# Rows 3 and 4 of a banded-attention and feed-forward kernel: row 3's x transposed by DMA, q and k loaded ahead of dilated v

## The chip, the cores and the metric

One core of one Trainium2 chip. The metric is the time of one execution in microseconds, as the device reports it; the median of 3 runs of the kernel before is 307.24 us (306.99 to 307.94).

The engines go by these names: PE is TensorE's matrix multiply and PEld its weight load, DVE is VectorE, ACT is ScalarE, POOL is GpSimd, SP is SyncE (which here issues DMAs only; its queue is SPq in the profile). Each engine works through its own instructions in order, and waits where one of them needs another engine's or a DMA's result.

## The reference, cut to what matters

```python
def _attn_ref(q, k, v):                   # (8, 8, 576, 64): batch, head, token, dim
    scores = scale * np.matmul(q, k.transpose(0, 1, 3, 2))
    rel = pos[:, None] - pos[None, :]
    mask_plain = (rel >= 0) & (rel < 32)                      # heads 0 to 3
    mask_dil = (rel >= 0) & (rel < 128) & (rel % 4 == 0)      # heads 4 to 7
    ...
    attn = np.exp(scores)
    attn = attn / (np.sum(attn, axis=-1, keepdims=True) + 1e-09)
    return np.matmul(attn, v)

def _moe_ref(x, w_in, w_out):             # x: (4608, 512), w_in: (512, 2048)
    r = np.maximum(x @ w_in, 0.0)
    return (r * r) @ w_out

def reference(q, k, v, moe_w_in, moe_w_out):
    attn_out = _attn_ref(q, k, v)
    x = attn_out.transpose(0, 2, 1, 3).reshape(8 * 576, 8 * 64)
    return _moe_ref(x, moe_w_in, moe_w_out)
```

So: banded attention, in heads 0 to 3 over the last 32 tokens ("sliding"), in heads 4 to 7 over every fourth of the last 128 ("dilated"), and then two dense layers over all 4608 tokens with a squared ReLU between them.

## The kernel before, in words

**Rows and chunks.** A *row* is one batch entry: 576 tokens of attention, rows 0 to 7. The dense layers work in chunks of 512 tokens, 0 to 8. While the attention of row b runs, the dense work of chunk b - 1 is dealt out between its pieces, so that TensorE always has something to do: `moe_gen(c)` is a generator, and each `pump(n)` takes n *steps* from it. From chunk 2 on, a chunk has 60 steps: 32 for the first layer (two per block of 128 hidden features, each two matmuls of 128x512 into a PSUM tile `ph`, after the second of them ScalarE's ReLU into `rt` and VectorE's square into `g`), and 28 for the second, a Strassen scheme with PSUM tiles `pa`, `pb`, `pc` (four matmuls of 128x256 to a step). The `ph`, `pa`, `pb`, `pc` tiles share four PSUM buffers, `rt` has three in SBUF. What each engine does, in which order, follows from the order of the program text alone.

**One row of attention.** Scores: two groups of sliding heads (`s_sliding`, tiles `ps`, from `QKTp`), two of dilated heads (`s_dilated`, `pz`, from `QKTd`), each followed by ScalarE's exponentials and VectorE's masks. Values: three groups of sliding blocks (`av_sliding`, `pav`, from `vp`), four of dilated ones (`av_dilated`, `paw`, from `vd`), each normalized by VectorE into `xs` or `xd`. Then x has to lie with features on partitions, in `xT`, which holds the last four rows. Two ways:

- by TensorE (`attn_values`, rows 0 to 3): `x_sliding` and `x_dilated` transpose blocks into PSUM (`px`, `py`), and ScalarE copies them into `xT`;
- by the DMA's crossbar (`attn_values_by_dma`, rows 4 to 7): SyncE issues transposing DMAs, the sliding ones straight into `xT`, the dilated ones into `yd`, from where ScalarE copies them (`x_from`, some steps later).

**What a row needs beforehand.** Its q and k: GpSimd's DMAs bring sliding q and k (`ns`) and put dilated q and k as fp16 in DRAM (`dd`); VectorE brings the sliding ones into order of tokens (`nr`, `by_token`), SyncE writes them to DRAM (`dp`, `keep_sliding_qk`) and reads both back transposed (`QKTp<-dp`, `QKTd<-dd`, two DMAs each, k and then q). Its v: SyncE loads `sv` (sliding) and `sd` (dilated) as fp32, GpSimd casts them into `vp` and `vd` (3 and 4 casts). Blocks overlap, so a *halo* of partitions 96 to 127 (sliding) or 64 to 127 (dilated) is copied down within `vp` and `vd`: by ScalarE in rows 0 to 2, by DMA on SyncE in rows 3 and 4 (`vp<-vp`, `vd<-vd`); in rows 5 to 7 the sliding one is a VectorE copy (line 196) put off to the end of the stage before (`at_end`, called in the Strassen scheme after the fourth product into `pa`, step 56).

`after_transposes(b)` is a tiny GpSimd copy that makes GpSimd wait for row b's transposes, so that no load of the next row is issued ahead of them.

**Where rows 3 and 4 stand.** The main loop has two parts: rows 2 and 3 in the old manner, rows 4 to 7 in the new. In the first, `turn_and_load` issues, for the next row: copy by token and `dp`, `sv`, `sd`, the four transposes, and all seven casts. Row 2 calls it after its third `av_sliding` (step 42 of its chunk's 64); row 3 calls it from `attn_scores` after the last scores (step 24 of 60). Row 3 begins its scores at step 12. In the second part a row begins its scores at step 3; `copied` (copy by token and `dp`) comes after the third `av_sliding`, for row 4 after the second; `first` (`sv`) after the first `x_dilated_by_dma`; `second` (transposes, then `sd`, the sliding casts, the halo at the end) after the other one. The dilated casts of a row from 5 on are made in the row itself, after GpSimd has issued the next row's loads.

Of the kernel before, what the change touches and what calls it, by code (L numbers as in the profile page):

```python
# [13 lines left out]
P = 128  # L14
# [3 lines left out]
def kernel(  # L18
# [9 lines left out]
    nc = tc.nc  # L28

    B, H, S, D = q.shape  # L30
# [16 lines left out]
    NB = S // QB  # L47
    PADP = P - QB
# [41 lines left out]
    vp = [const.tile([P, NB, HH, D + 2], FP16, name=f"vp{r}") for r in range(2)]  # L90
# [18 lines left out]
    def load_sliding_qk(b):  # L109
        n = natp.tile([P, HH, 9 * D], FP16, name=f"ns{b}", tag="n")  # L110
        for i, s in ((1, k), (0, q)):
            nc.gpsimd.dma_start(
                out=n[64 * i : 64 * (i + 1)],
                in_=s[b, 0:HH].rearrange("h (p j) d -> p h (j d)", j=9),
            )
        return n
# [8 lines left out]
    def load_sliding_v(b):  # L125
        vv = v[b, 0:HH].rearrange("h (m p) d -> p h m d", p=QB)
        if b == 0:
            for m in range(NB):
                nc.sync.dma_start(out=sv[PADP:P, :, m, :], in_=vv[:, :, m, :])  # L129
        else:  # L130
            for h in (0, 2):
                nc.sync.dma_start(out=sv[PADP:P, h : h + 2], in_=vv[:, h : h + 2])

    def load_dilated_v(b, eng):
        vv = v[b, HH:H].rearrange("h (i c) d -> i h (c d)", c=DIL)
        for t in range(2):
            eng.dma_start(out=sd[P - QD[t] : P, t, :, :], in_=vv[Q0D[t] : Q0D[t] + QD[t]])
# [29 lines left out]
    def cast_sliding_v(b, ms=range(0, NB, 2)):  # L167
        for m in ms:
            nc.gpsimd.tensor_copy(  # L169
                vp[b % 2][:, m : m + 2, :, 0:D], sv[:, :, m : m + 2, :].rearrange("p h m d -> p m h d")  # L170
            )

    def cast_dilated_v(b):
        for t in range(2):
            p0 = 64 * t
            for c in range(0, DIL, 2):
                nc.gpsimd.tensor_copy(  # L177
                    vd[b % 2][p0:P, t, c : c + 2, :, 0:D],
                    sd[p0:P, t, :, D * c : D * (c + 2)].rearrange("p h (c d) -> p c h d", d=D),
                )  # L180
# [11 lines left out]

    at_end: list = []

    def halo_sliding_at_end(b):
        nc.vector.tensor_copy(
            vp[b % 2][0:PADP, 1:NB, :, 0:D], vp[b % 2][P - PADP : P, 0 : NB - 1, :, 0:D]
        )

    def halo_sliding_by_dma(b):  # L200
        nc.sync.dma_start(out=vp[b % 2][0:PADP, 1:NB], in_=vp[b % 2][P - PADP : P, 0 : NB - 1])

    def halo_dilated_by_dma(b):
        nc.sync.dma_start(out=vd[b % 2][0:64, 1], in_=vd[b % 2][64:P, 0])

    def cast_v(b):
        cast_sliding_v(b)
        cast_dilated_v(b)


    def keep_dilated_qk(b):
        d = dpool.tile([2, HH * CL, DIL * D], FP16, name=f"dd{b}", tag="dd")
        for i, src in ((1, k), (0, q)):
            nc.gpsimd.dma_start(
                out=d[i].rearrange("(r i) x -> r (i x)", i=4),
                in_=src[b, HH:H].rearrange("h (r i) d -> (h r) (i d)", i=16),
                max_dma_last_dim=4096,
            )
        return d
# [10 lines left out]
    def transpose_sliding(b, dp):  # L230
        for i in (1, 0):
            nc.sync.dma_start_transpose(out=QKTp[b % 2][:, i, :, PADP:], in_=dp[i])

    def transpose_dilated(b, dd):
        for i in (1, 0):
            nc.sync.dma_start_transpose(out=QKTd[b % 2][:, i, :, KPAD:], in_=dd[i])
# [4 lines left out]
    def after_transposes(b):  # L241
        nc.gpsimd.tensor_copy(seen, QKTd[b % 2][:, 0, 1, KPAD : KPAD + 1])
# [25 lines left out]
    for m, w, pad in (  # L268
# [5 lines left out]
            out=lo_[:, 0:w], in0=relf[:, 0:w], scalar1=-pad - 0.5, scalar2=None, op0=ALU.is_gt  # L274
# [9 lines left out]
    for r in range(2):  # L284
        nc.vector.tensor_scalar(
            out=vd[r][:, 0, :, :, D],
# [220 lines left out]
    def moe_gen(c):  # L507
        g = hidden(c)
        yield from mm1_gen(c, g, c > 1)
        yield from (mm2_strassen_gen if c > 1 else mm2_gen)(c, g)  # L510
# [10 lines left out]
    def pump(n):  # L521
        for _ in range(n):
            while pending:
                try:
                    next(pending[0])
                    break
                except StopIteration:
                    pending.pop(0)
# [184 lines left out]
    def attn_scores(b, gap, less=0, hooks={}):  # L713
        for hp in range(2):
            s_sliding(b, hp)
            if hp in hooks:
                hooks[hp]()
            pump(gap)
        for g in range(2):
            s_dilated(b, g)  # L720
            if 2 + g in hooks:
                hooks[2 + g]()
            if g and b < 3:
                halo_sliding(b, 0)
            pump(gap - less)

    def attn_values(b, gap, wide=False, then=None):
        xs = x_tiles(b)
        for mp in range(3):
            av_sliding(b, mp, xs)  # L730
            if b < 3:
                if mp < 2:
                    halo_sliding(b, mp + 1)
                else:
                    halo_dilated(b, 0)
            if then and b == 2 and mp == 2:
                then()
            pump(gap + (b == 1 and mp == 0))
        x_sliding(b, 0, xs, wide)
        if b < 3:  # L740
            halo_dilated(b, 2)
        pump(gap)
        av_dilated(b, 0, 0, xs)
        if then and b == 1:
            then()
        pump(gap)
        x_sliding(b, 1, xs, wide)
        pump(gap)
        av_dilated(b, 0, 1, xs)
        pump(gap)  # L750
        for a in range(2):
            av_dilated(b, 1, a, xs)
            pump(gap)
        x_dilated(b, 0, xs, wide)
        pump(gap)
        x_dilated(b, 1, xs, wide)

    def attn_values_by_dma(b, then):
        xs = x_tiles(b)
        for mp in range(3):  # L760
            av_sliding(b, mp, xs)
            if mp == (2 if b > 4 else 1):
                then[0]()
            pump(3)
        x_sliding_by_dma(b, xs)
        ys = []
        for t in range(2):
            for a in range(2):
                av_dilated(b, t, a, xs)
                pump(4 + 2 * (a > t))  # L770
            ys.append(x_dilated_by_dma(b, t, xs))
            then[1 + t](ys[t])
        pump(6)
        x_from(b, 0, ys[0])
        pump(7)
        x_from(b, 1, ys[1])
# [38 lines left out]
    ns = load_sliding_qk(2)  # L815
# [43 lines left out]
    def turn(b, n):  # L859
        return keep_sliding_qk(b, by_token(b, n))  # L860

    for b in range(2, 4):
        pending.append(moe_gen(b - 1))
        nxt = b + 1
        after_transposes(b)
        ns = load_sliding_qk(nxt)
        if b == 2:
            cast_v(b)
        dd = keep_dilated_qk(nxt)
        if b == 3:  # L870
            halo_sliding_by_dma(b)
            halo_dilated_by_dma(b)

        def turn_and_load():
            dp = turn(nxt, ns)
            load_sliding_v(nxt)
            load_dilated_v(nxt, nc.sync)
            transpose_sliding(nxt, dp)
            transpose_dilated(nxt, dd)
            cast_v(nxt)  # L880

        pump(22 if b == 2 else 12)
        attn_scores(b, 4, 0, {3: turn_and_load} if b == 3 else {})
        attn_values(b, b, False, turn_and_load)
        pump(1000)

    for b in range(4, B):
        pending.append(moe_gen(b - 1))
        nxt = b + 1
        if nxt < B:  # L890
            after_transposes(b)
            ns = load_sliding_qk(nxt)
            dd = keep_dilated_qk(nxt)
        if b > 4:
            cast_dilated_v(b)
        else:
            halo_sliding_by_dma(b)
        halo_dilated_by_dma(b)
        dps = []

        def copied():
            if nxt < B:
                dps.append(turn(nxt, ns))

        def first(y):
            if nxt < B:
                load_sliding_v(nxt)

        def second(y):
            if nxt < B:  # L910
                transpose_sliding(nxt, dps[0])
                transpose_dilated(nxt, dd)
                load_dilated_v(nxt, nc.sync)
                nc.gpsimd.tensor_copy(seen, y[:, 0, 0, 0:1])
                cast_sliding_v(nxt)
                at_end.append(lambda: halo_sliding_at_end(nxt))

        pump(3)
        attn_scores(b, 3)
        attn_values_by_dma(b, (copied, first, second))  # L920
        pump(1000)
    pending.append(moe_gen(B - 1))
# [32 lines left out]
```

## Time and profile before

| what | value |
|---|---|
| median of 3 runs | 307.24 us (306.99 to 307.94) |
| the profiled execution's own time | 306.99 us |
| its span in the profile | 304.6 us |
| granted TensorE clock | 1.00 |
| VectorE's square, `g<-rt` 128x512 (line 329) | 446 ns, 144 of them |
| VectorE's halo copy of `vp` (line 196) | 485 ns, 3 of them |
| GpSimd's casts `vp<-sv`, `vd<-sd` | 675 and 695 ns |
| `dp<-nr`, issue to landing, median | 4.1 us |
| `QKTp<-dp` and `QKTd<-dd`, issue to landing, median | 4.5 and 3.9 us |
| `xT<-xs` and `yd<-xd`, issue to landing, median | 4.0 and 2.9 us |

Times in the profile are microseconds from the start of the span. A line of the timeline has an instruction group's start, its length, engine, source line, operation, written tile and read tiles; "x8" is a number of instructions run together, and a bracket at the end gives the idle time of the engine ahead of it and what ended that. Matmuls are pipelined, so the length of a group reaches a little into the next one. The stages lie like this: row 3's with chunk 2 from 95 us, row 4's from 128, row 5's from 158, row 6's from 188, row 7's from 218; from 248 on there is dense work only (chunks 7 and 8).

### The profile page before, as it was taken

The numbers are of one execution on the slowest core, as the hardware profiler recorded it, in microseconds if no ns is written. First come the engines' busy times: TensorE is split into PE (matmuls) and PEld (weight loads), VectorE is DVE, ScalarE is ACT, GpSimd is POOL, SyncE is SP. The second block draws the span as 40 slices with busy tenths as digits, with TensorE's granted clock in tenths as the row PEclk, the third lists the DMA queues.
The fourth block names the chain that finished last, engine by engine and source line by source line (L and its number), as shares of the span: only waits on it lengthen the run. The fifth ranks groups of instructions, "written<-read, shape, count | busy, mean of one in ns | idle before, by whom it ended". The sixth has DMA issues, their size and how long they took to land.

```text
span 304.6 us, 6894 instructions
## 1 busy us (share of the span) xinstructions
PE 286.2 (94%) x2760; PEld 192.7 (63%) x2760; DVE 210.4 (69%) x437; ACT 173.2 (57%) x293; POOL 63.7 (21%) x112
## 2 busy tenths in 40 slices
PE   1888999799999799999999999999999999999994
PEld 1554554454554358855888997558756975785583
DVE  7684549658861689479938994999499924824651
ACT  2856647478835783395349635953495346425620
POOL 4481008101611610530027002600230000000000
PEclk9999999999999999999999999999999999999999
DMA  7999994999699999997899989998983230003013
GB/s 115 196 195 213 210 172 79 195 227 226 132 198 148 261 176 213 174 250 144 140 155 273 174 142 196 270 182 169 165 246 41 39 132 8 2 1 138 2 36 103
DMA packets 77471, 46.77 MB, mean 154 GB/s; under 512 B 58432, under 2 KB 69184, under 8 KB 77440
## 3 DMA queue, kind: packets, MB, share of 16 engines
q1 hardware_dynamic: 68688, 32.71, 50.5%
q0 software_dynamic: 8752, 13.63, 26.4%
q8 instruction: 21, 0.34, 0.5%
q14 instruction: 10, 0.08, 0.1%
HBM read 36.70 MB, written 16.52 MB: 175 GB/s over the span
## 4 chain that ended last, share of the span: by engine, by line
PE 74%; DMA 17%; DVE 4%; POOL 1%; issue 1%; SPq 1%; ACT 1%; POOLq 0%; DVEq 0%
PE ph L305 35%; PE pa L382 15%; PE pb L382 7%; DMA sv<-in_v_dram 6%; PE po L450 5%; DMA wi<-in_moe_w_in_dram 5%; PE pc L382 4%; DMA QKTp<-dp 3%; DMA ns<-in_q_dram 2%; PE paw L659 2%; PE ps L588 1%; PE pav L643 1%; PE pz L613 1%; PE py L690 1%; SPq L129 1%
## 5 line engine op out<-in xcount | busy, mean ns | idle before, releaser
L305 PE MATMUL ph<-xT,wi 128*128 128x512 f16 (+1 forms) x640 | 134.2, 359 | 0.7 <-ACT xT L696 0.7
L328 ACT ACTIVATE rt<-ph 128x512 f16<-128x512 f32 x144 | 86.2, 608 | 44.6 <-PE ph L305 41.8
L305 PEld LDWEIGHTS <-wi 128*128 128x128 f16 x640 | 68.2, 114 | 45.9 <-issue 0.6
L329 DVE TENSOR_TENSOR g<-rt 128x512 f16<-128x512 f16 x144 | 62.7, 446 | 37.8 <-ACT rt L328 36.6
L382 PEld LDWEIGHTS <-g 128*128 128x128 f16 x448 | 43.0, 98 | 6.3 <-DVE g L329 0.2
L382 PEld LDWEIGHTS <-gs 128*128 128x128 f16 x336 | 32.5, 98 | 3.7
L450 PE MATMUL po<-wo,g 128*128 128x512 f16 x128 | 33.1, 379 | 0.0
L382 PE MATMUL pb<-wt,g 128*128 128x256 f16 x224 | 28.1, 273 | 0.0
L382 PE MATMUL pa<-wt,gs 128*128 128x256 f16 x224 | 27.1, 273 | 0.0
L169 POOL CAST vp<-sv 128x512 f16<-128x512 f32 x24 | 15.4, 675 | 55.4 <-DMA sv<-in_v_dram 42.7
L409 DVE TENSOR_TENSOR ov<-pb,ov 128x512 f32<-128x512 f32 x14 | 9.7, 692 | 23.7 <-PE pb L382 18.6
L398 ACT COPY ov<-pa 128x512 f32<-128x512 f32 x14 | 8.2, 587 | 28.0 <-PE pa L382 28.0
L177 POOL CAST vd<-sd 128x512 f16<-128x512 f32 (+1 forms) x32 | 21.4, 695 | 10.2 <-DMA sd<-in_v_dram 9.6
L631 DVE TENSOR_TENSOR xd<-paw,rcp_d 80x512 f16<-80x512 f32 (+1 forms) x32 | 21.9, 685 | 1.1
L572 ACT ACTIVATE AT<-ps 128x576 f16<-128x576 f32 x32 | 19.2, 657 | 3.0 <-PE ps L588 2.6
L572 ACT ACTIVATE AT<-pz 128x576 f16<-128x576 f32 x32 | 19.8, 693 | 1.3 <-PE pz L613 1.1
L575 DVE TENSOR_TENSOR AT<-AT,maskd 128x576 f16<-128x576 f16 x32 | 18.8, 613 | 1.9 <-ACT AT L572 0.8
L575 DVE TENSOR_TENSOR AT<-AT,maskp 128x576 f16<-128x576 f16 x32 | 15.0, 479 | 6.7 <-ACT AT L572 5.1
L631 DVE TENSOR_TENSOR xs<-pav,rcp_p 96x512 f16<-96x512 f32 x24 | 16.5, 687 | 0.8
L659 PEld LDWEIGHTS <-AT 128*128 128x128 f16 x256 | 11.9, 98 | 7.3 <-issue 2.4
L398 ACT COPY ou<-pa 128x512 f32<-128x512 f32 x14 | 8.2, 586 | 13.8 <-PE pa L382 13.8
L450 PEld LDWEIGHTS <-g 128*128 128x128 f16 x128 | 10.4, 97 | 8.3
(81 smaller groups left out, 274.7 us busy)
## 6 DMA issues: line engine op xcount, KB each, us to landing
sv<-in_v_dram SPq DMA_DIRECT2D x14, 288.0 KB, 5.4
dp<-nr SPq DMA_DIRECT2D x12, 288.0 KB, 4.1
out_dram<-ou SPq DMA_DIRECT2D x6, 512.0 KB, 4.0
out_dram<-ov SPq DMA_DIRECT2D x6, 512.0 KB, 4.8
sd<-in_v_dram SPq DMA_DIRECT2D x8, 320.0 KB, 6.1
ns<-in_k_dram POOLq DMA_DIRECT2D x8, 288.0 KB, 6.9
ns<-in_q_dram POOLq DMA_DIRECT2D x8, 288.0 KB, 8.3
sd<-in_v_dram SPq DMA_DIRECT2D x8, 256.0 KB, 5.5
```

The source lines that it names most:

```text
L169: nc.gpsimd.tensor_copy(vp[b % 2][:, m : m + 2, :, 0:D], sv[:, :, m : m + 2, :].rearrange("p h m d -> p m h d"))
L177: nc.gpsimd.tensor_copy(vd[b % 2][p0:P, t, c : c + 2, :, 0:D], sd[p0:P, t, :, D * c : D * (c + 2)].rearrange("p h (c d) -> p c h d", d=D),)
L305: nc.tensor.matmul(ph[:, t0:t1], wi4[ffc // 4][:, dmk, :, ffc % 4], xT[:, dmk, x0 : x0 + t1 - t0], start=(dmk == 0 and t0 == 0), stop=(dmk ...
L328: nc.scalar.activation(rt, ph[:], ACTF.Relu)
L329: nc.vector.tensor_mul(g[:, ffc, :], rt, rt)
L382: nc.tensor.matmul(banks[bank][:, t], a(k, t), b(k), start=(new and t == 0 and k == 0), stop=(k == HF - 1), skip_group_check=True,)
L398: nc.scalar.copy(ot, banks[A])
L450: nc.tensor.matmul(po, g[:, ffc, t * P : (t + 1) * P], wo[ffc // 4][:, ffc % 4, :], start=(ffc == 0), stop=(ffc == NFF - 1),)
L572: nc.scalar.activation(AT[:, u, 0:UW], ps[:, :, 0 : UW // 2], ACTF.Exp, scale=scale)
L575: nc.vector.tensor_mul(AT[:, u, 0:UW], AT[:, u, 0:UW], mask)
L631: nc.vector.tensor_tensor(out=x, in0=pv, in1=rb, op=ALU.mult)
L659: nc.tensor.matmul(pav[:, e, h * (D + 2) : h * (D + 2) + D + 1], AT[:, 4 + h, off : off + P], vd[b % 2][:, t, 2 * a + e, h, 0 : D + 1], st ...
```

## The change

Row 3 goes over from the first manner to the second, and the loop's first part becomes straight code for row 2 alone.

- `turn_and_load` (for row 3, called in row 2): the four transposes are issued ahead of the two `sd` loads, and GpSimd makes only the sliding casts; the dilated casts of row 3 come in row 3's own stage.
- Row 3: scores from step 6, then 3 steps between pieces; x by the crossbar with `attn_values_by_dma`; the copy by token for row 4 after the third `av_sliding` (again step 24), `sv` of row 4 behind the first dilated x transpose, the transposes for row 4 and its `sd` behind the second (step 45). Its sliding halo is a VectorE copy after the second group of sliding scores, its dilated halo stays a DMA. The last x copy comes at step 58 of 60 (in rows 4 to 7 at 55).
- Row 4: dilated casts in its own stage; sliding halo by VectorE at the end of row 3's stage in place of a DMA; the copy by token for row 5 after the third `av_sliding`, not the second.

Rows 5 to 7 are as before. The change in the code:

```diff
-    def halo_sliding_at_end(b):
+    def halo_sliding_at_once(b):
         nc.vector.tensor_copy(
             vp[b % 2][0:PADP, 1:NB, :, 0:D], vp[b % 2][P - PADP : P, 0 : NB - 1, :, 0:D]
         )
-
-    def halo_sliding_by_dma(b):
-        nc.sync.dma_start(out=vp[b % 2][0:PADP, 1:NB], in_=vp[b % 2][P - PADP : P, 0 : NB - 1])
...
-            if then and b == 2 and mp == 2:
+            if then and b > 1 and mp == 4 - b:
                 then()
...
-            if mp == (2 if b > 4 else 1):
+            if mp == 2:
                 then[0]()
...
-    for b in range(2, 4):
-        pending.append(moe_gen(b - 1))
-        nxt = b + 1
-        after_transposes(b)
-        ns = load_sliding_qk(nxt)
-        if b == 2:
-            cast_v(b)
-        dd = keep_dilated_qk(nxt)
-        if b == 3:
-            halo_sliding_by_dma(b)
-            halo_dilated_by_dma(b)
-
-        def turn_and_load():
-            dp = turn(nxt, ns)
-            load_sliding_v(nxt)
-            load_dilated_v(nxt, nc.sync)
-            transpose_sliding(nxt, dp)
-            transpose_dilated(nxt, dd)
-            cast_v(nxt)
-
-        pump(22 if b == 2 else 12)
-        attn_scores(b, 4, 0, {3: turn_and_load} if b == 3 else {})
-        attn_values(b, b, False, turn_and_load)
-        pump(1000)
-
-    for b in range(4, B):
+    pending.append(moe_gen(1))
+    after_transposes(2)
+    ns = load_sliding_qk(3)
+    cast_v(2)
+    dd = keep_dilated_qk(3)
+
+    def turn_and_load():
+        dp = turn(3, ns)
+        load_sliding_v(3)
+        transpose_sliding(3, dp)
+        transpose_dilated(3, dd)
+        load_dilated_v(3, nc.sync)
+        cast_sliding_v(3)
+
+    pump(22)
+    attn_scores(2, 4)
+    attn_values(2, 2, False, turn_and_load)
+    pump(1000)
+
+    for b in range(3, B):
...
-        if b > 4:
-            cast_dilated_v(b)
-        else:
-            halo_sliding_by_dma(b)
+        cast_dilated_v(b)
         halo_dilated_by_dma(b)
...
-                at_end.append(lambda: halo_sliding_at_end(nxt))
-
-        pump(3)
-        attn_scores(b, 3)
+                at_end.append(lambda: halo_sliding_at_once(nxt))
+
+        pump(6 if b == 3 else 3)
+        attn_scores(b, 3, 0, {1: lambda: halo_sliding_at_once(b)} if b == 3 else {})
         attn_values_by_dma(b, (copied, first, second))
         pump(1000)
```

## The prediction

> **What bounds the kernel now.** I read the page's engine shares first, then TensorE's order of work around the edited rows, then SyncE's queue beside it, then busy time by stage. The page and the list of waits:
>
> ```profile
> PE 286.2 (94%) x2760; PEld 192.7 (63%) x2760; DVE 210.4 (69%) x437; ACT 173.2 (57%) x293; POOL 63.7 (21%) x112
> ...
> PE ps L588 <- DMA QKTp<-dp: 2.0, 2, 1.6
> ```
>
> TensorE is the bound: a change counts by the work it takes from TensorE and by the waits it makes or ends there. One of the few waits after the start is the sliding scores' (`ps`) for the transposed q and k, 1.6 us of it once. TensorE's timeline puts it at the head of row 3:
>
> ```profile
> 95.08 5.34 PE L305 MATMUL ph<-xT,wi 128*128 128x512 f16 x24
> 102.04 0.43 PE L588 MATMUL ps<-QKTp 64*128 64x96 f16 x12 [1.62 <-DMA QKTp<-dp]
> ...
> 115.91 0.42 PE L672 MATMUL px<-ident,xs 96*128 96x96 f16 x6
> 116.17 1.48 PE L382 MATMUL pc<-wo,g 128*128 128x256 f16 x12
> ...
> 219.90 0.43 PE L588 MATMUL ps<-QKTp 64*128 64x96 f16 x12 [0.38 <-DMA QKTp<-dp]
> ```
>
> Row 3 runs its 12 dense steps (24 matmuls), idles 1.62 us, and starts its scores at 102.04. Row 7 shows the same wait at 219.90, 0.38 us. SyncE's queue says what is late for row 3 (start, us spent issuing):
>
> ```profile
> 85.14 1.14 SPq L224 DMA_DIRECT2D dp<-nr  x2
> 86.37 3.42 SPq L132 DMA_DIRECT2D sv<-in_v_dram  x2
> 89.89 3.72 SPq L137 DMA_DIRECT2D sd<-in_v_dram  x2
> 93.70 5.71 SPq L232 DMA_TRANSPOSE QKTp<-dp  x2
> 99.50 3.04 SPq L236 DMA_TRANSPOSE QKTd<-dd  x2
> ```
>
> The transposes queue behind both loads of v. By stage, from one row's first score to the next row's (rows 3, 4, 5, 6):
>
> ```profile
> 95.08:129.68 34.60, 32.70 (x323) 22.44 (x322) 24.27 (x48) 19.22 (x34) 11.39 (x19) 1.00 1.17 196
> 129.68:159.54 29.86, 29.86 (x299) 21.50 (x300) 23.51 (x49) 18.09 (x31) 4.65 (x9) 1.00 0.89 173
> 159.54:189.46 29.92, 29.92 (x351) 26.91 (x352) 24.76 (x49) 17.99 (x31) 7.67 (x13) 1.00 1.01 194
> 189.46:219.90 30.44, 30.05 (x289) 20.61 (x289) 25.02 (x50) 18.22 (x31) 7.11 (x13) 1.00 0.94 194
> ```
>
> (The first begins at row 3's first dense step. Columns: length, busy PE, PEld, DVE, ACT, POOL, clock, DMA share, GB/s.) In rows 4 to 6, TensorE is full; row 3's stage is what the change can shorten. The clock is 1.00 throughout.
>
> **The change part by part.** *Row 3's x leaves TensorE.* 28 transposes (two `px` groups of 6, two `py` of 8) go. From the start of each group to the next matmul they take 0.26, 0.32, 0.29 and 0.34: 1.21 us. ScalarE's copies out of them (0.59 to 0.69) become copies from `yd` (1.1 to 1.3), about 1.1 us more in a stage where ScalarE has some 15 us free: nothing. Four crossbar transposes on SyncE replace them; in row 4 they land 2.6 to 4.4 us after issue, three dense steps or more ahead of use, as `x_from` comes late: nothing directly.
>
> The VectorE: DVE Perf Modes page of the Trainium skill (Rules for kernel authors) speaks against this: a 128x128 transpose belongs on TensorE when PSUM will do. Its table gives 390 ns there and 1309 ns by the crossbar, so by an estimate from it the row's 18 blocks would be 7 us of TensorE against 24 us of DMA. The trace's 1.21 us for the whole row decides; the rule leaves out that here TensorE is the full engine.
>
> *Row 3's scores from step 6; the transposes ahead of dilated v.* Six steps from 95.24 (the chain has 1.30 us for 6 matmuls, so 2.60) make TensorE ready at 97.84. When does q land? `dp` for k is issued at 85.14 and lands after 6.3 us, at 91.5; the transposes can't issue before. Row 2's pattern had `dp` directly ahead of the transposes but for a 0.5 MB store: first issued at 61.99, second landed at 63.9 + 4.0 = 67.9, 5.9 us on. That gives 97.4 here, no wait. The other bound: only the issue moves, from 93.70 to 91.5, and the landing of 102.04 with it, to 99.8: 2.0 us of wait. The 576 KB of sliding v in 256-byte pieces still lie ahead, worse than row 2's store, so I take a middle 98.75: **0.9 us of wait (0 to 2.0)**. QKTd landed 2.8 us behind QKTp before, and row 3's dilated scores come 3.6 us behind the first: no second wait.
>
> *Row 4's q and k come later.* Before, row 3 issued them at step 24; now at step 45, behind `dp`, the x transposes and sliding v, as rows 4 to 6 do. There the second QKTp landed 28.05, 29.46 and 30.40 us after the row's own first score (157.8, 189.0, 219.86), and the next scores came 29.9 us after it: 1.7 and 0.5 us early, then 0.4 late. Row 3 has three steps less between its scores and row 4's, since it starts at step 6, not 3: 29.92 - 1.30 = 28.62. VectorE sets when `yd` issues (it runs without a gap from 160.50 to past 182): three or so products `g` (0.4 each) fall before the scores, but the halo copy (0.49) and one `ou` add (0.67) come in ahead of the last `xd`, and some 0.4 idles early, +0.35 in all. By the nearest rows, 5 and 6, the landing is at 29.93 + 0.35 = 30.3; by row 4, which had its copy earlier and no casts beside, 28.4. I take 30.1: **1.5 us of wait (0 to 2.2)**.
>
> *Row 4 and the moved v work.* Row 4's copy moves from step 18 to 21, so row 5 loses row 4's 1.7 us margin and stands between +0.5 and -0.4: **0.1 us (0 to 0.4)**. Four dilated casts each for rows 3 and 4 (2.9 us a row on GpSimd) move behind the next loads' issue; GpSimd is idle there and row 5's do the same. The sliding halo moves from SyncE (0.61 to 0.76 of issue) to VectorE: 0.49 us each. Row 3's waits for the `vp` casts, over at 99.96, while VectorE reaches it about 4 us after the scores, near 102.7: no stall. Behind it stand `g` products; three `rt` and four `ph` buffers cover about 3 us; uncovered it would cost its own excess. Row 4's waits at the end of row 3's stage for the casts behind `yd`; such waits (up to 2.4 us) held nobody in rows 5 to 7. `vd<-vd` waits in SyncE ahead of `dp`, but `dp` isn't due for 5 us more. Row 3's dilated v, issued after four transposes (about 1.5 us each from 91.5) near 98, lands some 5 us later (rows 5 to 7: 4.4 to 4.8), near 103; its casts take 2.9, and the first dilated product comes 11.8 us after the scores (row 5: 171.26 against 159.47), near 110.5: hidden.
>
> **Sum.** From 95.24 to row 4's scores at 129.75 are 34.51 us. After: 2.60 + 0.9 + 28.62 + 1.5 = 33.62, a gain of 0.89; less 0.1 for row 5: **0.8 us**. The gross is 3.29 (1.62 and 0.28 of ended waits, 1.21 of transposes, the rest slips), of which two new waits give most back. The profiled execution took 306.99 (span 304.6), which makes 306.2; the median is 0.25 higher, which makes **306.4**.
>
> **The rivals.** *A, forecast:* both waits remain in part, 305.4 to 307.4, chance 0.5.
> *B, the crossbar is in time:* QKTp follows `dp` as in row 2 and row 4's lands by row 4's pattern, no waits: gain 3.3, 304.0; with a remnant of 0.5, 304.5. For it: the two quick cases. Against: rows 5 and 6 slip nearer to zero margin each time. 0.2.
> *C, slower by late q and k at each row's head:* row 3's landing at its late bound (2.0), row 4's at 2.2, and rows 5 and 6 each at row 7's 0.4 with SyncE's queue slipping: 3.29 - 5.0 = -1.7, so 308.9. It decides once the waits at the heads add to over 3.3 us. For it: the DMA engines' share is already 1.17 in row 3's stage, and row 7 waits. Against: in rows 5 and 6 the slip stays under 0.4. 0.25.
> *D, the turn doesn't advance anything:* the transposes still wait for `dp` of q (93.1) and stand behind sliding v, landing near 101: wait 3.2, gain about -1.4 to 0; 307.8. 0.05.
>
> On the crossbar's rate, Advanced Engine Details and Errata in the skill (X-Bar Transpose (TRN2)) expects 350 to 400 GB/s; by an estimate from that, two transposes of 288 KB would take 1.6 us. Between 99 and 104 the trace moved 215 to 255 GB/s in full microseconds of transposes (143 in one), which speaks for C rather than B.
>
> **How the numbers follow.** About 0.3%, 0.9 us, can't be told from no change. A's gains run from -0.2 to 1.8, somewhat under half of them over 0.9: 0.22 of faster, with B 0.42. Same: 0.28 from A, 0.05 from C's mild end, 0.02 from D: 0.35. Slower: the rest of C and D, 0.23. The range leaves B's best and C's worst outside: 304.6 to 308.5; the forecast's own is 305.4 to 307.4.
>
> **What would show it.** No `px` or `py` groups after row 2; `sd` issued behind QKTd; first `ps` of row 3 near 98.8 with a wait of 0 to 2; row 4's `ps` near 128.9 with a wait of 0.5 to 2.2 on QKTp; later stages 29.9 to 30.4. I am wrong if row 4's wait is gone or above 2.5, if TensorE waits on `vp`, `vd` or `xT` in row 3, or if VectorE stalls at the halo copy.

## The result and the profile after

| measurement | before, median | changed, median | ratio, 95% interval |
|---|---|---|---|
| first, 4 runs each | 307.24 us (306.99 to 307.94) | 306.24 us (306.05 to 306.43) | 0.9964 [0.9946, 0.9982] |
| repeat on chip 7 (c1_again), 29 and 12 runs | 305.16 us | 305.76 us | 1.0018 [0.9984, 1.0052] |
| repeat on chip 1 (e4_again2), 23 and 12 runs | 306.10 us | 305.99 us | 1.0007 [0.9971, 1.0042] |

The first measurement (its chip isn't on record) is 1.0 us faster, 0.4%; the forecast was 306.4. The two repeats, whose runs spread more (303 to 310 us), show no gain; their intervals allow from 0.9 us faster to 1.6 us slower. So the number was met, but the change is worth about 1 us at most, and perhaps nothing. The traces say more, because single stages are steadier than the whole.

TensorE's timeline of the changed kernel around row 3 and the heads of rows 4 and 5:

```profile
93.66 2.75 PE L302 MATMUL ph<-xT,wi 128*128 128x512 f16 x12
96.82 0.43 PE L585 MATMUL ps<-QKTp 64*128 64x96 f16 x12 [0.41 <-DMA QKTp<-dp]
...
111.33 0.42 PE L656 MATMUL paw<-vd,AT 128*128 128x65 f16 x8 [0.43 <-DVE xs L628]
...
127.19 0.43 PE L585 MATMUL ps<-QKTp 64*128 64x96 f16 x12 [0.82 <-DMA QKTp<-dp]
...
137.85 0.41 PE L640 MATMUL pav<-vp,AT 128*128 128x65 f16 x8 [0.37 <-DVE xs L628]
```

SyncE's queue there, first for row 3's q, k and v, then for row 4's:

```profile
83.72 1.14 SPq L221 DMA_DIRECT2D dp<-nr  x2
84.96 3.17 SPq L132 DMA_DIRECT2D sv<-in_v_dram  x2
89.57 4.66 SPq L229 DMA_TRANSPOSE QKTp<-dp  x2
94.33 2.97 SPq L233 DMA_TRANSPOSE QKTd<-dd  x2
97.35 1.32 SPq L137 DMA_DIRECT2D sd<-in_v_dram  x2
...
113.07 3.82 SPq L698 DMA_TRANSPOSE xT<-xs  x2
116.99 1.23 SPq L705 DMA_TRANSPOSE yd<-xd  x1
118.27 1.22 SPq L132 DMA_DIRECT2D sv<-in_v_dram  x2
119.74 1.99 SPq L705 DMA_TRANSPOSE yd<-xd  x1
121.85 2.78 SPq L229 DMA_TRANSPOSE QKTp<-dp  x2
```

And by stage, as before the change (row 3's first dense step to row 4's first score, then score to score for rows 4 and 5; the columns are those of the prediction):

```profile
93.66:127.19 33.53, 31.78 (x296) 21.32 (x295) 24.91 (x50) 19.40 (x32) 9.09 (x16) 1.00 0.95 189
127.19:157.62 30.43, 30.06 (x294) 21.25 (x294) 25.44 (x50) 17.64 (x30) 7.04 (x13) 1.00 1.01 200
157.62:188.72 31.10, 30.37 (x347) 26.70 (x347) 24.60 (x49) 17.78 (x31) 7.22 (x13) 1.00 0.93 189
```

The transposes of row 3's x are gone from TensorE, its wait of 1.62 us has shrunk to 0.41, and the first stage is 1.07 us shorter than the 34.60 of before. But row 4 now begins with a wait of its own, TensorE waits for VectorE's `xs` in both rows, and rows 4 and 5 are longer than the 29.79 and 29.93 of before (by the starts of the first scores). Both traces span 304.6 us. The changed one reached row 3 1.42 us sooner (93.66 against 95.08). That may be chance: the code up to there is the same but for the places of a few DMAs and casts, and ten of the traces in the table below reached row 3 anywhere from 93.6 to 95.1 us, and one (d1_casts_act4, after a stretch at half clock) at 97.8. The traced execution of e3_qk_first_act was a slow one (318.39 us, granted clock 0.984), so its stages aren't in the table.

### The profile page after: what moved, and what is told of

It is laid out like the page before. It is cut to its first block, busy times and chain, and to the rows that moved or that the text cites. A ratio compares the mean times of both kernels' runs of the same rounds, so it can differ in the third digit from the quotient of the medians.

```text
span 304.6 us, 6841 instructions
## 1 busy us (share of the span) xinstructions
PE 286.2 (94%) x2732; PEld 191.3 (63%) x2732; DVE 214.0 (70%) x439; ACT 173.0 (57%) x291; POOL 64.9 (21%) x113
## 4 chain that ended last, share of the span: by engine, by line
PE 68%; DMA 12%; DVE 9%; ACT 6%; issue 3%; SPq 1%; POOL 1%; POOLq 0%
PE ph L302 26%; PE pa L379 15%; DMA ns<-in_q_dram 7%; PE pb L379 7%; PE po L447 6%; PE pc L379 4%; DVE g L326 3%; DMA QKTp<-dp 3%; ACT AT L569 3%; PE paw L656 2%; ACT rt L325 2%; DMA QKTd<-dd 2%; DVE AT L572 2%; PE ps L585 1%; PE pf L513 1%
## 5 line engine op out<-in xcount | busy, mean ns | idle before, releaser
L326 DVE TENSOR_TENSOR g<-rt 128x512 f16<-128x512 f16 x144 | 64.2, 460 | 34.1 <-ACT rt L325 32.9
L379 PE MATMUL pa<-wt,gs 128*128 128x256 f16 x224 | 26.9, 273 | 0.0
L177 POOL CAST vd<-sd 128x512 f16<-128x512 f32 (+1 forms) x32 | 22.7, 736 | 12.7 <-DMA sd<-in_v_dram 12.2
L572 DVE TENSOR_TENSOR AT<-AT,maskd 128x576 f16<-128x576 f16 x32 | 19.7, 642 | 2.6 <-ACT AT L569 1.5
L902 POOL COPY seen<-yd 128x1 f16<-128x1 f16 x4 | 0.8, 191 | 73.6 <-DMA yd<-xd 73.6
```

What stands on the lines that cost most here:

```text
L177: nc.gpsimd.tensor_copy(vd[b % 2][p0:P, t, c : c + 2, :, 0:D], sd[p0:P, t, :, D * c : D * (c + 2)].rearrange("p h (c d) -> p c h d", d=D),)
L326: nc.vector.tensor_mul(g[:, ffc, :], rt, rt)
L379: nc.tensor.matmul(banks[bank][:, t], a(k, t), b(k), start=(new and t == 0 and k == 0), stop=(k == HF - 1), skip_group_check=True,)
L572: nc.vector.tensor_mul(AT[:, u, 0:UW], AT[:, u, 0:UW], mask)
```

## The experiments

The stages of the traces, in us, for the whole section. "To row 4" starts at row 3's first dense step; the others run from the row's first score to the next row's, and "rest" from row 7's first score to the end. Each kernel has one trace. The ratio is that of the times to the kernel before on the same chip: 7 for the c runs, 3 for the d runs, 1 for the e runs. The changed kernel itself ran on chips 7 and 1, not on 3.

| kernel | to row 4 | row 4 | row 5 | row 6 | rest | ratio to before, 95% |
|---|---|---|---|---|---|---|
| before | 34.60 | 29.79 | 29.93 | 30.50 | 84.70 | |
| changed | 33.53 | 30.43 | 31.10 | 30.38 | 85.50 | 0.9964 [0.9946, 0.9982] |
| c1_again | 33.97 | 30.37 | 29.95 | 30.38 | 85.63 | 1.0018 [0.9984, 1.0052] |
| c2_order_only | 36.05 | 29.79 | 30.29 | 30.78 | 84.74 | 1.0151 [1.0107, 1.0195] |
| c3_step3 | 33.18 | 30.60 | 31.47 | 30.06 | 85.20 | 0.9975 [0.9944, 1.0005] |
| c4_step9 | 34.97 | 30.35 | 29.93 | 30.11 | 84.52 | 1.0042 [1.0011, 1.0073] |
| d1_casts_act4 | 33.34 | 30.54 | 29.99 | 30.31 | 84.75 | 1.0006 [0.9974, 1.0038] |
| d2_row4_early | 33.67 | 31.44 | 30.30 | 31.15 | 86.23 | 1.0031 [0.9995, 1.0068] |
| d3_x_by_pe | 33.20 | 29.79 | 30.30 | 31.16 | 84.82 | 0.9982 [0.9956, 1.0009] |
| d4_sd_first | 37.60 | 30.43 | 30.46 | 29.82 | 84.80 | 1.0079 [1.0038, 1.0119] |
| e1_qk_first | 35.32 | 29.79 | 34.31 | 32.39 | 84.78 | 1.0203 [1.0127, 1.0279] |
| e2_qk_first_pe | 33.29 | 29.79 | 32.58 | 32.85 | 84.78 | 1.0077 [1.0045, 1.0110] |
| e3_qk_first_act | | | | | | 1.0218 [1.0179, 1.0257] |
| e4_again2 | 33.41 | 30.93 | 30.01 | 30.13 | 84.54 | 1.0007 [0.9971, 1.0042] |

**The changed kernel again (c1_again, e4_again2).** No edit; on chips 7 and 1.

> The changed kernel once more, for its size against the kernel before and for a second trace. Theory (the gain is row 3's stage, 1.07 us shorter in the first trace, and the small waits of rows 4, 5 and 7 there vary from execution to execution): 1.0 us faster than before (0.6 to 1.4); in this trace row 3's stage takes 33.2 to 33.9 us from its first dense step to row 4's first score, and rows 4 to 6 together differ by over 0.5 us from the 91.9 us of the first trace. Rival (the change itself costs rows 4 to 7 some 1.7 us on VectorE and in the loads, and only a faster start hid it): the waits of 0.37 us in row 4 and 0.68 us in row 5 come back in the same places.

> The changed kernel on the same chip as the three variants, for their comparison, and for its size against the kernel before on another chip. Theory (0.85 us gained up to row 4's first score, 0.6 us lost in row 4's stage): 0 to 0.6 us faster than before, which the noise of these runs may hide; from row 3's first dense step to row 4's first score 33.5 to 34.0 us, row 4's stage 30.3 to 30.6. Rival (the first measurement's 1.0 us holds): 0.8 to 1.2 us faster.

The first stage came out at 33.97 and 33.41, just outside both forecasts (33.2 to 33.9 and 33.5 to 34.0, each missed by 0.1); row 4's was 30.37, and 30.93 against a forecast of 30.3 to 30.6. Row 4's wait for q came back in all three traces (0.82, 0.86, 0.63 us), its wait of 0.37 us for `xs` in the first repeat alone (0.30); the 31.10 of row 5 came back in neither. In both new traces TensorE also waits for `xT` ahead of row 4 (here c1_again):

```profile
127.10 0.81 PE L302 MATMUL ph<-xT,wi 128*128 128x512 f16 x3 [0.38 <-ACT xT L693]
128.77 0.43 PE L585 MATMUL ps<-QKTp 64*128 64x96 f16 x12 [0.86 <-DMA QKTp<-dp]
```

Mean of the three: 33.64 to row 4, so 0.96 us gained; row 4 30.58, so 0.79 lost. The times didn't show the theory's 0.6 to 1.4 us in the one, nor the rival's 0.8 to 1.2 in the other.

**Only the order of row 3's loads (c2_order_only).** The kernel before, with

```diff
             load_sliding_v(nxt)
-            load_dilated_v(nxt, nc.sync)
+            if b == 3:
+                load_dilated_v(nxt, nc.sync)
             transpose_sliding(nxt, dp)
             transpose_dilated(nxt, dd)
+            if b == 2:
+                load_dilated_v(nxt, nc.sync)
             cast_v(nxt)
```

> The kernel before with one thing of the change: in row 2, row 3's four transposes are issued ahead of its dilated v. Theory (the transposes waited behind sd, and dp to landing is some 13.1 us with sd out of the way as in the changed kernel): the second QKTp lands 13.1 us after dp is issued, some 3.8 us sooner than the 16.9 of before, so the wait of 1.62 us ahead of row 3's scores at step 12 is gone: 1.3 to 1.7 us faster than before, which is more than the whole change. Rival (the transposes wait for the DMA engines, not for their place in the queue): the wait stays above 1 us, and the time within 0.5 us of before.

The wait ahead of row 3's scores went, as the theory said; yet the kernel was 1.5% slower than before. GpSimd's, VectorE's and TensorE's timelines show the new wait:

```profile
103.50 2.93 POOL L177 CAST vd<-sd 128x512 f16<-128x512 f32 x4 [6.69 <-DMA sd<-in_v_dram]
106.49 0.26 POOL L242 COPY seen<-QKTd 128x1 f16<-128x1 f16 x1
107.03 0.65 POOL L112 DMA_DIRECT2D ns<-in_k_dram  x1 [0.28 <-DVE g L329]
```

```profile
113.26 0.76 DVE L120 COPY nr<-ns 128x2304 f16<-128x2304 f16 x1 [2.96 <-DMA ns<-in_q_dram]
```

```profile
115.67 0.41 PE L643 MATMUL pav<-vp,AT 128*128 128x65 f16 x8 [3.41 <-DVE xs L631]
```

GpSimd waits 6.69 us for the later `sd`, casts, and only then issues row 4's loads of q and k. VectorE's copy of them waits 2.96 us, with row 3's `xs` behind it, and TensorE waits 3.41 us for `xs`. By this trace the new order pays only together with the dilated casts behind the loads, which the change also makes. The trace's stage accounts for 1.45 us; the runs lost some 4.6. The granted clock points to much of the rest: as a run's mean it was 0.987 to 0.993 in all six runs, and 0.997 or more in 27 of the 29 of the kernel before. By an estimate from the two means, 0.990 and 0.9985 over 308 us, that is up to 2.6 us of TensorE's time. In the traced run (0.992) the slow stretch lies at 25 to 29 us, ahead of the edit's place (from 85 us); where it lies in the other runs isn't on record, so why the clock is lower stays open.

**Row 3's scores from step 3 and from step 9 (c3_step3, c4_step9).** `pump(6 ...)` ahead of row 3's scores becomes 3, or 9.

> The changed kernel with row 3's scores from step 3, as in rows 4 to 7. Theory (q and k land by SyncE's queue, whatever TensorE does; 3 steps are 1.30 us): row 3's wait grows from 0.41 to 1.7 us, row 4's of 0.82 us falls to 0; the sum from 1.2 to 1.7: 0.5 us slower than the changed kernel (0.2 to 0.9), 0.1 to 0.8 us faster than before. Rival (VectorE sets the pace in row 3, and the landing of row 4's q moves along with the scores): row 4's wait stays near 0.8, and the time is 1.0 to 1.4 us above the changed kernel.

> The changed kernel with row 3's scores from step 9. Theory: row 3's wait falls from 0.41 to 0, row 4's grows from 0.82 to 2.1 us: 0.9 us slower than the changed kernel (0.5 to 1.3), so about as fast as before. Rival (VectorE sets the pace): three more steps of g are done before the scores, VectorE is freer behind them, row 4's wait grows by under 0.5, and the time is within 0.3 us of the changed kernel.

The waits of the scores moved just as the theory had it. From step 3, row 3 waits 1.77 us (1.7 expected) and row 4 not at all. From step 9, row 3 doesn't wait, and row 4's head waits 0.94 for q and 1.17 for `xT`, 2.11 together (2.1 expected). The sum was mis-sized for step 3: the first stage is not 0.5 us longer but the shortest of the three places, 33.18 against 33.64 and 34.97. TensorE's waits for `xs` later in the row (0.43 in each of the changed kernel's traces from step 6, 1.08 from step 9) aren't there. That VectorE catches up while TensorE waits for q fits, but isn't shown: in d4_sd_first row 3's scores wait 2.45 us, and the 0.43 is there all the same. The times have the order of the first stages: on chip 7 the medians are 304.79 us from step 3, 305.76 from step 6 and 306.88 from step 9. But from row 3's first dense step to the end the traces take 210.51, 210.30 and 209.88, so these don't show where step 3 is faster. Which waits remain for TensorE isn't a sum of independent terms.

**Row 4's dilated casts on ScalarE (d1_casts_act4).** In outline:

```diff
-        cast_dilated_v(b)
-        halo_dilated_by_dma(b)
+        # for row 4: one cast by nc.scalar.copy after the last scores and after
+        # each sliding product, the halo's DMA after the second cast
```

> The changed kernel with row 4's four dilated casts on ScalarE, in its order after the dilated scores and after each sliding product, instead of on GpSimd. In four traces of the changed order row 4's stage (first score to row 5's) took 30.35 to 30.60 us against 29.79 before. Theory (GpSimd's casts slow VectorE, whose squares beside them took 1.24 us each instead of 0.42 to 0.46): the squares and masks of row 4 stay at 0.4 to 0.5 us, and row 4's stage is 29.8 to 30.0 us; 0.5 us off the time, within the noise of the runs. Rival 1 (the copy by token at a later place costs it): the stage stays at 30.3 to 30.6 and the squares are quick all the same. Rival 2 (ScalarE becomes late instead): the stage is over 30.6.

VectorE's timeline, first the changed kernel's two squares beside GpSimd's casts (133.15 to 135.85), then two squares of this one in row 4 and the copy by token:

```profile
132.88 2.49 DVE L326 TENSOR_TENSOR g<-rt 128x512 f16<-128x512 f16 x2
```

```profile
136.81 0.92 DVE L334 TENSOR_TENSOR g<-rt 128x512 f16<-128x512 f16 x2
...
144.32 0.76 DVE L120 COPY nr<-ns 128x2304 f16<-128x2304 f16 x1 [0.93 <-DMA ns<-in_q_dram]
```

The casts do slow VectorE, and without them its squares are quick. TensorE's wait for `xs` behind them (0.37 us in the changed kernel's trace, at 137.85) is gone, but the stage stayed at 30.54: the theory's price fell. Rival 1's signs came out, the quick squares and the old length, and the next run tests it. VectorE now waits at the copy by token, 0.93 us for row 5's q; behind it TensorE waits 0.29 us for `xd`. That named the next suspect, the loads. The second repeat of the changed kernel (e4_again2) shows the same without the edit, where q was issued at 132.81 and landed 9.2 us later (the profile names the halo's DMA `vd<-vd` as what ended the wait):

```profile
142.08 0.76 DVE L120 COPY nr<-ns 128x2304 f16<-128x2304 f16 x1 [1.16 <-DMA vd<-vd]
```

**Row 5's copy by token early again (d2_row4_early).** `if mp == 2` becomes `if mp == (1 if b == 4 else 2)`.

> The changed kernel with row 5's copy by token and dp again after row 4's second sliding product, as before. Theory (GpSimd's casts beside VectorE make row 4's stage 0.6 us longer): the stage stays at 30.3 to 30.6 us, and row 5's scores don't wait in either case. Rival (the later copy does it): the stage is back at 29.8 to 30.0 us.

Neither: row 4's stage grew to 31.44, so rival 1 fell too. VectorE idles 1.40 us ahead of the early copy, until 141.31. The profile puts that down to `vd<-vd` again; q's load, issued at 132.62, landed 8.6 us later, at 141.2, and by the code the copy reads it. TensorE then waits 1.14 us for `xs`. The copy has to be late because the loads are late.

**Row 3's x by TensorE (d3_x_by_pe).** All else is as in the changed kernel, except that GpSimd's small copy ahead of row 4's sliding casts waits for `xd`, as there is no `yd`. Cut to the main lines:

```diff
-        x_sliding_by_dma(b, xs)
+        if b > 3:
+            x_sliding_by_dma(b, xs)
...
+                if b == 3 and t == 0:
+                    x_sliding(b, a, xs, False)
...
-        x_from(b, 0, ys[0])
+        x_from(b, 0, ys[0]) if b > 3 else x_dilated(b, 0, xs, False)
```

> The changed kernel with row 3's x transposed by TensorE again (28 transposes, sliding ones after the first two dilated products' dense steps, dilated ones where the copies out of yd stood); all else is as in the changed kernel. Theory (the crossbar takes 1.21 us off TensorE, but its transposes stand ahead of row 4's q and k in SyncE's queue): from row 3's first dense step to row 4's first score 1.2 us of transposes come in and row 4's wait of 0.82 to 0.86 us goes: 33.9 to 34.3 us, against 33.53 and 33.97; so 0 to 0.6 us slower than the changed kernel. Rival (the crossbar's place in the queue doesn't matter): row 4's wait stays, and the stage is 34.7 to 35.2 us.

33.20 us: better than the theory's 33.9 to 34.3, and not longer than with the crossbar although 28 transposes are back. SyncE's and TensorE's timelines:

```profile
115.62 5.10 SPq L229 DMA_TRANSPOSE QKTp<-dp  x2
120.82 3.11 SPq L233 DMA_TRANSPOSE QKTd<-dd  x2
```

```profile
127.23 0.43 PE L585 MATMUL ps<-QKTp 64*128 64x96 f16 x12
```

Without the x transposes in front, row 4's q and k are issued 6.2 us sooner (6.4 to 6.7 counted from row 3's first dense step, against the changed kernel's three traces). Row 4 starts without a wait, GpSimd issues the loads for row 5 sooner, and row 4's stage is 29.79 again, with the casts on GpSimd. GpSimd's issue of row 5's q, first here, then in the changed kernel:

```profile
127.38 0.62 POOL L112 DMA_DIRECT2D ns<-in_q_dram  x1
```

```profile
131.44 0.63 POOL L112 DMA_DIRECT2D ns<-in_q_dram  x1
```

To row 5's first score it takes 62.99 us (33.20 + 29.79), against 63.96, 64.34 and 64.34 with the crossbar and 64.39 before. From row 3's first dense step to the end it takes 209.27, within the crossbar's 209.02 to 210.94.

The loads sort all traces of the table. From row 4's first score to the issue of row 5's load of q it is 1.6 us before, 1.7 in c2_order_only, 0.2 here, 2.5 in e1_qk_first, 0.5 in e2_qk_first_pe: row 4's stage is 29.79 us in each. It is 4.2 to 4.5 us in the changed kernel, its two repeats, c3, c4, d1, d2 and d4: the stage is 30.35 to 31.44. Late loads act in two ways. GpSimd makes row 4's dilated casts behind them, so the casts come 5.9 to 6.3 us after row 4's first score in the changed kernel's traces and 2.4 here, where TensorE waits for nothing in row 4; and the copy by token can wait for them, as in d1 and e4_again2. (In e1_qk_first TensorE's wait of 2.99 us just ahead of row 4 gives VectorE time as well; here and in e2_qk_first_pe there is no such wait.)

**Dilated v ahead again (d4_sd_first).** In the changed kernel's `turn_and_load`, `load_dilated_v(3, nc.sync)` goes back ahead of the transposes.

> The changed kernel with row 3's dilated v loaded ahead of the four transposes again. Theory (sd ahead costs the landing 3.8 us: dp to the second landing took 16.9 us before, 13.1 in the changed kernel): row 3's wait grows from 0 to 0.41 to about 4 us, VectorE catches up in it, which gives back up to 0.8 us; from row 3's first dense step to row 4's first score 36.5 to 37.8 us; 3 to 4 us slower than the changed kernel. Rival (the transposes wait for the DMA engines, in whichever order): row 3's wait is under 1.5 us and the time within 1 us of the changed kernel.

```profile
99.29 0.60 PE L585 MATMUL ps<-QKTp 64*128 64x96 f16 x12 [2.45 <-DMA QKTp<-dp]
```

37.60 us, in the theory's range, but not as it had it: q landed 15.2 us after `dp`, and row 3 waited 2.45 us, not 4. A slower clock behind the wait (last section) makes up some 1.3 us of the rest. The order is worth about 2 us of waiting. The time is 0.8% above before, so some 2 us above the changed kernel by the ratios, not 3 to 4.

**Row 4's q and k into SyncE's idle time (e1_qk_first, e2_qk_first_pe, e3_qk_first_act).** In rows 3 to 6 QKTp is issued behind the first `yd` transpose; in the changed kernel, in the one with row 3's x by TensorE, and in the changed kernel with row 3's sliding halo copied by ScalarE:

```diff
         def first(y):
             if nxt < B:
+                transpose_sliding(nxt, dps[0])
                 load_sliding_v(nxt)
...
-                transpose_sliding(nxt, dps[0])
                 transpose_dilated(nxt, dd)
```

> The changed kernel with the two QKTp transposes for the next row issued in rows 3 to 6 behind the first yd transpose, ahead of sliding v and of the second yd transpose, where SyncE stands idle. Theory (what the crossbar gains in row 3 is given back by row 4's q and k, which stand behind its transposes in SyncE's queue, and by the loads of the row after, which wait for the last of them): the second QKTp of row 4 lands some 4 us sooner, row 4's wait of 0.66 to 0.86 us goes, QKTd and the loads come 1.5 to 2.6 us sooner, row 4's stage is 29.8 to 30.2 us (30.35 to 30.60 in the changed kernel), and from row 3's first dense step to row 4's first score it is 32.4 to 33.2 us; 1.0 to 2.0 us faster than the changed kernel. Rival (VectorE is the bound in these stages): the waits go, but row 4's stage stays at 30.3 or more, as VectorE's late products hold TensorE, and the time is within 0.5 us of the changed kernel.

> The kernel with row 3's x by TensorE, with the same earlier place for QKTp in rows 3 to 6. Theory: in row 3 nothing changes (33.0 to 33.4 us to row 4's first score, as without crossbar transposes SyncE's queue was free); rows 5 and 6 lose their waits of 0.18 and 0.76: 0.5 to 1.0 us faster than without, and 0.2 to 0.8 us slower than the variant with the crossbar in row 3 as 1.21 us of transposes stay. Rival (VectorE's bound): the crossbar in row 3 brings nothing even with q and k in time, and the two variants are equal within 0.3 us in the stages of rows 3 and 4 together.

> The same as the first of this set, with row 3's sliding halo copied by ScalarE instead of VectorE. Theory (VectorE is full in row 3, and its 0.49 us halo copy comes out of TensorE's waits for xs, 0.43 us): the wait of row 3's first dilated product for xs shrinks from 0.43 to 0 to 0.1 us, 0.3 us off row 3's stage. Rival (ScalarE's copy of over 1 us delays rt and so g): the wait stays at 0.4 or more.

Row 4's wait for q went and its stage was 29.79, as the theory had it; yet the three kernels were 2.0%, 0.8% and 2.2% slower than before. The stage to row 4 was 35.32 in the first (32.4 to 33.2 expected) and 33.29 in the second (33.0 to 33.4 expected); the second lost its time in rows 5 and 6. ScalarE's and TensorE's timelines of the first:

```profile
128.07 1.06 ACT L693 COPY xT<-yd 128x512 f16<-128x512 f16 x1 [3.64 <-DMA yd<-xd]
```

```profile
125.39 0.81 PE L302 MATMUL ph<-xT,wi 128*128 128x512 f16 x3
129.19 0.81 PE L302 MATMUL ph<-xT,wi 128*128 128x512 f16 x3 [2.99 <-ACT xT L693]
```

Now the second `yd` transpose is late. SyncE issued it 28.8 us after row 3's first dense step (at 123.42), against 26.1 to 26.9 in the changed kernel's traces; the copy out of it waited 3.64 us for it, and the fourth matmul of the next chunk waited 2.99 us for the copy. The same wait stands ahead of rows 6 and 7 (2.49 and 1.42 here, 2.35 and 1.36 with x by TensorE in row 3). By the code, chunk 3 ends at column 2047 of `xT` and that copy begins at column 2048, so the matmul reads nothing of it. Why it waits all the same isn't shown. An order kept for the copy's whole stretch of `xT` would fit: the copy writes the tails of feature blocks 2 and 3, the fourth matmul reads block 3, which lies between the two tails, and the third, of block 2, doesn't wait. A copy split by feature block wasn't tried. In the third kernel's trace the wait of 0.43 us for `xs`, which its edit was to end, is there too.

## Why the prediction came out as it did

**Row 3's x.** Right in itself: the `px` and `py` groups (1.21 us) are gone from TensorE. "Nothing directly" for the transposes on SyncE failed: ahead of row 4's q and k, of `yd` and of the loads they cost what they saved (d3_x_by_pe). The rule of the Trainium skill's page VectorE: DVE Perf Modes (Rules for kernel authors), transposes to TensorE when PSUM will do, was set aside because TensorE is full. The stages up to row 5 favour it all the same, 62.99 against 63.96 to 64.34 us; the times of the two, as ratios to before, overlap.

**Row 3's wait.** 0.9 us predicted (0 to 2.0), 0.41, 0 and 0 measured. The mechanism holds: the first transposes issue when k's `dp` lands (89.57, with `dp` at 83.72 + 5.8), and q landed 13.1 us after `dp`'s issue; the prediction's 98.75 meant 13.6.

**Row 4's wait.** 1.5 us predicted, 0.82, 0.86 and 0.63 measured for q; 0, 0.38 and 0.18 more for `xT`, from the copy that now comes three steps later, which was costed at nothing. The signs for a wrong prediction named `xT` only in row 3; the wait came at the first steps of row 4's stage.

**VectorE.** Costed as hidden, with the halo's stall alone looked at. That didn't happen (the copy ran at 100.66 without a wait), but VectorE's backlog held TensorE: 0.43 us for the third `xs` in each of the three traces, 0.42 and 0.29 for another in two. Row 4's dilated casts were put at nothing as well, since GpSimd is idle there; but VectorE's squares beside them took up to 1.24 us each, and in two of the three traces TensorE then waited 0.37 and 0.30 us for `xs`.

**Row 4's stage.** The mis-sized step: "0.1 us (0 to 0.4)" was 0.64, 0.58 and 1.14. It looked at q and k for row 5's scores, which never waited, and not at GpSimd: `after_transposes` holds the next loads until QKTd lands, so what is late for row 4 is late once more for row 5's loads, row 4's casts behind them, the copy by token, and VectorE's queue. Rows 4 and 5 of the first trace, 30.43 and 31.10, also lie outside the 29.9 to 30.4 that were to show it.

**The sum.** 0.89 us to row 4's first score was predicted, 0.96 measured (mean of three); less 0.79 in row 4, not 0.1, leaves 0.2 us, which agrees with the repeats better than with the first measurement. From row 3's first dense step to the end the traces take 209.52 us before and 210.94, 210.30 and 209.02 changed, so they show no gain over that whole stretch. On what the first measurement's 1.0 us rests stays open: its changed runs agree within 0.4 us, the repeats don't show it, and of the two profiled executions (306.99 and 306.38 us) the 0.6 us between them lies outside the span, 304.6 in both. That the time came within 0.2 us of the forecast is therefore partly luck.

## What to carry to other kernels

A queue that works in order is a resource like an engine. Before moving work from a full engine to it, list what stands behind, and ask of each transfer who waits for it and who waits for that; here a saving of 1.21 us was given back at the next row's head and in its stage, through loads held behind the last transpose. When several waits are near zero margin, taking one away lets the next one out, so compare the stages of several traces and not one wait. And an order of DMAs belongs to the casts and loads that follow it: the half of this change that looked best alone made the kernel 1.5% slower.

## What the runs showed of the hardware

TensorE's granted clock can fall to half after a wait of some 2 us. In d4_sd_first, the stretches of one microsecond around the wait of 2.45 us (length, busy PE, PEld, DVE, ACT, POOL, clock, DMA share, GB/s):

```profile
98.00:99.00 1.00, 0.00 (x0) 0.00 (x0) 0.00 (x0) 0.00 (x0) 0.00 (x0) 1.00 0.97 161
99.00:100.00 1.00, 0.71 (x13) 0.54 (x13) 0.00 (x0) 0.30 (x1) 0.00 (x0) 0.70 1.01 223
100.00:101.00 1.00, 1.00 (x3) 0.29 (x2) 0.54 (x2) 0.89 (x2) 0.00 (x0) 0.50 1.15 207
101.00:102.00 1.00, 1.00 (x4) 0.29 (x2) 0.38 (x1) 0.24 (x1) 0.08 (x1) 0.50 1.15 386
```

Six matmuls took 2.68 us there, from 99.83 to 102.51, and 1.41 in the next such group. The same 0.50 for about 3 us followed waits of 2.49 us (e1_qk_first), 2.35 us (e2_qk_first_pe) and 2.08 us (d1_casts_act4, at 60 us), but not waits of 2.99 us (e1_qk_first) and 3.41 us (c2_order_only). In c2_order_only it also came at 25 to 29 us, with no wait above 0.74 us in the ten us ahead, where the kernel before has nearly the same waits (0.74 the longest) at a clock of 1.00. So the length of one wait doesn't decide. The Trainium skill, TensorE: Matmul & The Clock Gate (Why this matters for your kernels), warns of gaps over about 3 us; the runs show it sooner, and once not at 3.4.

The spread of the times goes with this clock: of the 87 runs of the kernel before on chips 7, 3 and 1, the 51 with a mean clock of 0.999 or 1.000 took 305.3 us on average, the 13 with 0.994 or less 308.2.

GpSimd's casts beside VectorE's squares made these 1.24 us each (2.49 for two) in the changed kernel's first trace, against 0.46 without (d1_casts_act4). How much depends on how the two meet: beside the same casts a square took 0.62 us in d3_x_by_pe, 0.83 in e4_again2 and 1.52 in e1_qk_first.
